# Hash attention and Fourier mixing on one Trainium2 core: the first weight's column means taken in one run through DRAM, the first pair's keys loaded head by head, the projection asked for first, the first key-bit copies dealt out anew

## The chip, the cores and the metric

The kernel runs on one core of a Trainium2 chip. The metric is the device time of one launch in microseconds (us). A core has a matrix engine (TensorE, PE in the profile; its weight loads are PEld), a vector engine (VectorE, DVE), a scalar engine (ScalarE, ACT), GpSimd (POOL) and SyncE (SP), which here only issues DMA transfers. ACT and POOL issue some transfers too. Each engine runs its own list of instructions in order, and semaphores hold an instruction until its operands are ready.

## The reference

```python
def _attn_ref(q, k, v, proj):                       # q, k, v: (4, 8, 768, 64), proj: (64, 6)
    q_bits = np.einsum('bhsd,dk->bhsk', q, proj) > 0
    k_bits = np.einsum('bhsd,dk->bhsk', k, proj) > 0
    powers = 2 ** np.arange(n_bits)
    q_bucket, k_bucket = np.sum(q_bits * powers, axis=-1), np.sum(k_bits * powers, axis=-1)
    mask = q_bucket[:, :, :, None] == k_bucket[:, :, None, :]
    scores = np.where(mask, scale * np.matmul(q, k.transpose(0, 1, 3, 2)), -1e9)
    attn = softmax(scores)                          # denominator + 1e-09
    return np.matmul(attn, v)                       # -> x: (4, 768, 512)

def _moe_ref(x, w_ch1, w_ch2):                      # w_ch1: (512, 2048), w_ch2: (2048, 512), float64
    mixed = np.real(fft(fft(x, axis=1), axis=2))
    u = x + mixed
    un = (u - mean(u)) / sqrt(var(u) + 1e-06)       # over the last axis
    return u + np.maximum(un @ w_ch1, 0.0) @ w_ch2
```

## The kernel before, in words

There are two phases. The attention phase takes 16 pairs of heads (four batches of four pairs; `n` is the pair's number). The mixing phase then does the Fourier transforms and the two-layer network for the four batches. `_any_scores` is a second version for inputs with large scores, which is not entered with these inputs.

**A pair.** `load` fetches queries, keys and values. For every pair but the first, queries and keys come in 32-column strips (runs of 128 bytes), which DVE can transpose itself. For the first pair (`n == 0`) the rows come as they lie, with a head's row as a run of 256 bytes, half from SP's queue and half from ACT's, and PE transposes them (tiles `trq`, `trk`; `ident` is the identity); DVE and ACT copy the results to `qt` and `kt`. `prepare` also multiplies queries and keys by the projection (`pj`, filled by POOL from `pjr`), which gives `bits`; DVE thresholds them into `qb`; and six small copies put the key bits into `kk` (two halves for each head) and the second query half into `q1`. `scores` multiplies the bits (a mask term, line 848) and the true values (line 858) into one tile `sc`, and ACT takes the exponential into `pk`. `values` multiplies `pk` with `vn` into `oo`, and DVE adds the `pk` up in `acc` for the softmax's denominator.

**Steps beside a pair.** A pair has three passes (`v` = 0, 1, 2), each with the scores of two key blocks and then the values of the two blocks before. Between them `next(other)` runs one step of `weights1`, four steps a pair from pair 2 on. `weights1` fetches w1 (`zraw`, SP's queue) in 16 slices of 128 x 512, and turns float64 into float32 in two steps a slice (DVE lines 643, 647 and 657, ACT lines 651 to 654). After every fourth slice, with a block of 512 columns complete, `centred(f)` subtracts the column means (the network's input is normalised, so its mean can be taken out of the weight): `average` sums the four slices with `ones` on PE (tile `ws`, the four sums side by side in four groups of 32 rows), ACT copies the sums to `part`, a second product with the constant matrix `mean` adds the four parts and spreads the mean over all rows (tile `wm`), ACT copies it to `avg`, and DVE subtracts it from the four slices, two in a step (`centre`).

**What sets the order.** In the attention phase the order of the code is the order on PE, DVE, ACT, POOL and SP (`manual_schedule`). Score tiles and all other PSUM tiles of this phase take turns in three buffers. SP takes its transfers in order, and one that waits for its data or its buffer holds back those behind it. When w1's columns are centred, SP also stores parts of them (tile `ad`, line 1271) for the mixing phase.

**Start.** PE runs nine products with `mean` (tile `busy`) while the first loads are under way. POOL fills constants, copies `pjr` into `pj`, and then issues half of the second pair's loads of queries and keys.

Of the kernel before, what the change touches and what calls it, by code (L numbers as in the profile page):

```python
# [11 lines left out]
F32 = mybir.dt.float32  # L12
# [471 lines left out]
def _main(  # L484
# [55 lines left out]
    def load(n, names="qkv", second=nc.sync):  # L540
# [6 lines left out]
        for nm in names:  # L547
            src = {"q": q, "k": k, "v": v}[nm]
            tag, bufs = ("vn", 2) if nm == "v" else ("qkn", 4)
            tl = at_([P, S], F32, tag, f"{nm}n{n}", bufs)  # L550
            nat[nm, n] = tl
            if nm == "v" or n == 0:
                tc_ = tl.rearrange("p (c h d) -> p c h d", c=NT, h=2)
                for h in range(2):
                    s = src[b, 2 * t + h]
                    s = (
                        s.rearrange("(p c) d -> p c d", c=NT) if n == 0
                        else s.rearrange("(c p) d -> p c d", p=P)
                    )
                    (second if h else nc.sync).dma_start(tc_[:, :, h, :], s)  # L560
                continue
            for i in range(4):
                s = src[b, 2 * t + i // 2, :, i % 2 * 32 : i % 2 * 32 + 32]
                d = tl[32 * i : 32 * i + 32]
                if nm == "k":
                    (nc.gpsimd if n == 1 and i % 2 else nc.sync).dma_start(
                        d.rearrange("p (j a) -> p j a", a=32),
                        s.rearrange("(j b) a -> b j a", b=32),
                    )
                else:  # L570
                    s = s.rearrange("(j b r) a -> r b j a", b=32, r=2)
                    d = d.rearrange("p (r j a) -> r p j a", r=2, a=32)
                    for r in range(2):
                        (nc.gpsimd if n == 1 and r else nc.sync).dma_start(d[r], s[r])
# [16 lines left out]
    nc.gpsimd.memset(pj, 0.0)  # L591
    pjr = const.tile([P, NBITS], F32, tag="pjr", name="pjr")
    for h in range(2):
        nc.sync.dma_start(pjr[h * D : (h + 1) * D], proj)
    for io, i in ((0, 0), (0, 1), (1, 0), (1, 2)):
        nc.gpsimd.tensor_copy(pj[:, io, 1 + i * NBITS : 1 + (i + 1) * NBITS], pjr)
    cmp_ = const.tile([P, 2, 2], F32, tag="cmp", name="cmp")
# [18 lines left out]
    for i in range(2):  # L616
        kks.append(att.tile([P, S], BF16, tag=f"kk{i}", name=f"kk{i}"))
        q1s.append(att.tile([P, HALF], BF16, tag=f"q1{i}", name=f"q1{i}"))
        nc.gpsimd.memset(kks[i], 0.0)
        nc.gpsimd.memset(q1s[i], 0.0)  # L620
    sq = const.tile([P, 2, 2, HALF + 1], F32, tag="sq", name="sq")
    ch = const.tile([P, 2, 2, DM // 2], F32, tag="ch", name="ch")
# [43 lines left out]

    def average(f):


        ps = pt([P, WC], f"ws{f}")  # L670
        for c in range(NDC):
            nc.tensor.matmul(
                ps[32 * c : 32 * c + 32, :], ones, w1[:, c, f : f + WC],
                start=True, stop=True,
            )
        part = wt([P, WC], F32, "u", f"part{f}", 2)
        nc.scalar.copy(part, ps)
        yield
        ps = pt([P, WC], f"wm{f}")
        nc.tensor.matmul(ps, mean, part, start=True, stop=True)  # L680
        avg = wt([P, WC], F32, "u", f"avg{f}", 2)
        nc.scalar.copy(avg, ps)
        yield avg

    def centre(f, avg, cs):
        for c in cs:
            w = w1[:, c, f : f + WC]
            nc.vector.tensor_tensor(w, w, avg, op=ALU.subtract)

# [51 lines left out]

    def centred(f):

        avg = average(f)
        next(avg)
        yield
        ps = next(avg)
        yield
        for c in range(0, NDC, 2):
            centre(f, ps, (c, c + 1))  # L750
            yield

    def weights1():
# [7 lines left out]
        for i in range(len(slices)):  # L761
            low = wt([P, WC], I32, "u", f"low{i}")
            yield from arrival.convert(i, low)
            yield
            if i % NDC == NDC - 1:
                yield from centred(fs[i // NDC])

# [4 lines left out]
    def prepare(n):  # L772

        ts = {}
        for nm in "qk":
# [9 lines left out]
            for g in range(2) if n == 0 else ():  # L785
                ps = pt([P, 3, P], f"tr{nm}{n}_{g}")
                for i in range(3):
                    c = 2 * i + g if nm == "q" else 3 * g + i
                    nc.tensor.transpose(ps[:, i, :], tn[:, c * P : (c + 1) * P], ident)
                if nm == "q":  # L790
# [27 lines left out]
        for h in range(2):  # L818
            nc.vector.tensor_scalar(
                bits[:, h], pss[h], cmp_[:, h, 0:1], cmp_[:, h, 1:2],  # L820
                op0=ALU.is_gt, op1=ALU.mult,
            )
        for h in range(2):
            to = slice(64 * h, 64 * h + 32)
            rest = [(kk[to, 0:HALF], 2), (kk[to, HALF:S], 3), (q1[to], 1)]
            for dst, i in rest:
                i ^= 2 * h
                (nc.scalar.copy if h else nc.vector.tensor_copy)(
                    dst, bits[32 * i : 32 * i + 32, h]
                )  # L830
        preps[n] = ts["q"], ts["k"], (bits, q1), kk
# [38 lines left out]
    def values(n, c, pk, oos):  # L870

        for g in range(2):
            w = HALF + 1 - g
            for h in range(2):
                nc.tensor.matmul(  # L875
                    oos[g][h * D : (h + 1) * D, 0:w], nat["v", n][:, (2 * c + h) * D : (2 * c + h + 1) * D],
                    pk[:, g, h, 0:w], start=(c == 0), stop=(c == NT - 1),
# [1014 lines left out]
```

## Time and profile before

| | |
|---|---|
| median of 3 runs | 998.35 us (997.3 to 999.73) |
| the profiled execution | 997.41 us, of which 995.3 us is the span of the instructions |
| mean granted clock of TensorE | 0.999 |
| busy: PE, DVE, ACT, POOL | 983.4, 724.7, 481.7, 96.6 us |
| attention phase | from the start to about 338 us |

The span runs from the first to the last instruction; the 2.1 us left of the profiled execution lie around it. A view called the chain follows the work that ended last back from the end, and names what each piece waited for. Rows of the timeline give start, length, engine, line, tile and, in brackets, idle time before it and who ended it. A row with x16 stands for 16 instructions. A product in float32 shows as two passes on PE, so 4 products show as x8.

### The profile page before, as it was taken

The page shows a single profiled execution, that of the slowest core. Times are in us where ns is not written, and L with a number is a line of the kernel's source. Part 1 is how long each engine was busy: PE and PEld are TensorE (multiplying, and loading weights), DVE is VectorE, ACT ScalarE, POOL GpSimd, SP SyncE. Part 2 cuts the span into 40 slices and gives each one's busy share as a digit, 9 for nine tenths or more (in the row PEclk, how much of TensorE's full clock was granted, in tenths as well). Part 3 has the DMA queues.
Part 4 walks back from the last instruction along what each step waited for, and adds up shares of the span by engine and source line. Part 5 has one row for each costly group of instructions (what it writes and reads, how often), then busy time and mean ns, then how long its engine had stood idle before and what let it go on. Part 6 is the DMA issues. An engine that isn't in the chain of part 4 may idle for free.

```text
span 995.3 us, 15351 instructions
## 1 busy us (share of the span) xinstructions
PE 983.4 (99%) x5505; PEld 692.0 (70%) x5505; DVE 724.7 (73%) x1276; ACT 481.7 (48%) x933; POOL 96.6 (10%) x193
## 2 busy tenths in 40 slices
PE   8999999999999999999999999999999999999997
PEld 5444444444444666875896686799989999998986
DVE  4788898878987597877835487547898857793672
ACT  5787887878866466047034423221643531430420
POOL 3000000000000000421212130002310001200000
PEclk9999999999999999999999999999999999999999
DMA  9545373453620337576663577205848612743701
GB/s 143 128 91 111 77 164 68 96 112 85 142 57 17 125 105 265 178 225 217 210 231 116 159 236 278 79 16 179 269 131 267 203 38 75 250 126 105 229 33 46
DMA packets 207141, 141.37 MB, mean 142 GB/s; under 512 B 128464, under 2 KB 190416, under 8 KB 207056
## 3 DMA queue, kind: packets, MB, share of 16 engines
q1 hardware_dynamic: 196464, 106.48, 38.9%
q0 software_dynamic: 9024, 33.43, 10.9%
q8 instruction: 46, 0.75, 0.3%
q10 hardware_dynamic: 1568, 0.39, 0.2%
q14 instruction: 39, 0.32, 0.1%
HBM read 111.94 MB, written 28.31 MB: 141 GB/s over the span
## 4 chain that ended last, share of the span: by engine, by line
PE 92%; DVE 3%; DMA 2%; ACT 1%; POOL 1%; issue 1%; SPq 0%; DVEq 0%; POOLq 0%
PE o L1400 29%; PE oo L875 13%; PE h L1750 13%; PE sc L858 12%; PE h_px L1514 6%; PE h_p L1514 5%; PE sc L848 4%; PE cs L1073 3%; PE A L1102 2%; PE B L1102 2%; DMA zraw<-in_moe_w_ch_dram 1%; PE sum L895 1%; PE bits L812 1%; PE un L1192 1%; DVE x L1116 0%
## 5 line engine op out<-in xcount | busy, mean ns | idle before, releaser
L1400 PE MATMUL o<-w,h 128*128 128x256 f32 x768 | 177.6, 379 | 0.0
L865 ACT ACTIVATE pk<-sc 128x768 f32<-128x768 f32 x192 | 152.5, 813 | 34.9 <-PE sc L858 31.4
L1400 PEld LDWEIGHTS o<-w,h 128*128 128x128 f32 x768 | 145.2, 190 | 19.0
L858 PE MATMUL sc<-qt,kt 64*128 64x384 f32 x768 | 155.6, 482 | 0.0
L875 PE MATMUL oo<-pk,vn 128*64 128x385 f32 (+1 forms) x768 | 134.5, 492 | 0.0
L932 DVE TENSOR_TENSOR acc<-acc,pk 128x1536 f32<-128x1536 f32 x63 | 110.1, 1748 | 3.1
L875 PEld LDWEIGHTS oo<-pk,vn 128*64 128x64 f32 x768 | 50.9, 136 | 81.0 <-issue 79.1
L1400 PE MATMUL o<-w,tq 128*128 128x256 f32 x384 | 91.1, 380 | 0.4 <-DVE w L1412 0.4
L858 PEld LDWEIGHTS sc<-qt,kt 64*128 64x128 f32 x768 | 69.6, 189 | 30.5 <-issue 30.0
L1400 PEld LDWEIGHTS o<-w,tq 128*128 128x128 f32 x384 | 72.5, 190 | 11.2 <-DVE w L1412 1.3
L1426 ACT COPY tq<-o 128x256 f32<-128x256 f32 x24 | 8.9, 372 | 141.0 <-PE o L1400 141.0
L1412 DVE SCALAR_TENSOR_TENSOR w<-o,rs,w 128x256 f32<-128x256 f32 x88 | 41.5, 480 | 40.2 <-PE o L1400 39.5
L1750 PE MATMUL h<-sums,w 128*128 128x192 f32 x336 | 61.6, 330 | 0.0
L1750 PEld LDWEIGHTS h<-sums,w 128*128 128x128 f32 x336 | 55.0, 190 | 2.9 <-DVE h L1688 2.0
L848 PEld LDWEIGHTS <-kk 33*128 33x128 bf16 x384 | 19.7, 93 | 50.8 <-issue 28.6
L1750 PE MATMUL h<-x,w 128*128 128x192 f32 x256 | 49.5, 326 | 0.0
L1435 ACT COPY tq<-o 128x256 f32<-128x256 f32 x24 | 8.9, 372 | 74.9 <-PE o L1400 74.9
L1750 PEld LDWEIGHTS h<-x,w 128*128 128x128 f32 x256 | 42.9, 190 | 0.1
L1400 PE MATMUL o<-w 128*128 128x256 f32 x176 | 41.7, 380 | 0.5 <-DVE w L1381 0.5
L1750 PE MATMUL h<-w 128*128 128x192 f32 x192 | 38.5, 327 | 0.0
L1688 DVE TENSOR_TENSOR h<-h,h 128x384 f32<-128x384 f32 x52 | 27.8, 551 | 14.5 <-PE h L1750 13.2
L1685 ACT ACTIVATE h<-h 128x768 f32<-128x768 f32 (+1 forms) x40 | 27.7, 712 | 20.3 <-DVE h L1688 19.6
(210 smaller groups left out, 1639.7 us busy)
## 6 DMA issues: line engine op xcount, KB each, us to landing
w<-ad SPq DMA_DIRECT2D x252, 128.0 KB, 2.6
w<-bd SPq DMA_DIRECT2D x42, 512.0 KB, 4.8
zraw<-in_moe_w_ch_dram SPq DMA_DIRECT2D x16, 512.0 KB, 4.5
zraw<-in_moe_w_ch_dram POOLq DMA_DIRECT2D x16, 512.0 KB, 4.0
bd<-w SPq DMA_DIRECT2D x14, 512.0 KB, 4.6
vn<-in_v_dram SPq DMA_DIRECT2D x32, 192.0 KB, 3.1
qn<-in_q_dram SPq DMA_DIRECT2D x116, 48.0 KB, 3.3
kn<-in_k_dram SPq DMA_DIRECT2D x58, 96.0 KB, 3.0
```

What stands on the lines that cost most here:

```text
L848: nc.tensor.matmul(pss[g][:, h, 0:HALF], kk[r, ks], bits[1][r] if g else bits[0][r, h], start=start, stop=not start,)
L858: nc.tensor.matmul(pss[g][:, h, 0:HALF], kt[rows, ks], qt[rows, g * HALF : (g + 1) * HALF], start=early, stop=not early,)
L865: nc.scalar.activation(pk[:, g, :, 0:HALF], pss[g][:, :, 0:HALF], AF.Exp, scale=SCALE)
L875: nc.tensor.matmul(oos[g][h * D : (h + 1) * D, 0:w], nat["v", n][:, (2 * c + h) * D : (2 * c + h + 1) * D], pk[:, g, h, 0:w], start=(c == ...
L932: nc.vector.tensor_tensor(acc, (first[:, :, :, 0:HALF] if c == 1 else acc), new, op=ALU.add)
L1073: nc.tensor.matmul(ps[:, pc + 2 * lo : pc + 2 * hi - 1 : 2], z[:, cp, pc, par, t * P : (t + 1) * P], ch[:, cp, pc, lo:hi], start=(cp == 0) ...
L1102: nc.tensor.matmul(ps[:, cols], F[:, par, k, t, j * P : (j + 1) * P], sq[:, t, k, cols], start=(t == 0), stop=(t == 1),)
L1400: nc.tensor.matmul(ps, a[:, r], right7[i][:, r], start=start and r == 0, stop=r == HF // 2 - 1, skip_group_check=not start,)
L1412: done_by[ET.DVE] = nc.vector.scalar_tensor_tensor(t[:, cols], src, r, t[:, cols], op0=ALU.mult, op1=ALU.add)
L1514: nc.tensor.matmul(ps, left[:, k], right[i][:, k], start=start and k == 0, stop=k == 1, skip_group_check=not start,)
L1688: done_by[ET.DVE] = nc.vector.tensor_tensor(d, x, y, op=ALU.add)
L1750: nc.tensor.matmul(ps[at_bank][:, g], ring[n % NR][:, g], parts[i][j], start=start and g == 0, stop=g == 1, skip_group_check=True,)
```

## The change

Four edits.

1. `centred` is called once, after all 16 slices are converted. It sums all 16 slices in one run of 16 products into one tile (the four column blocks side by side, accumulated over the four slices of each), ACT copies the sums scaled by 1/512 to `part`, SP writes the four rows of means to a DRAM tile `md`, and each block's means come back spread over all 128 rows by a DMA into `avg`. The first two are asked for in the step after the write, three steps ahead of their use, the other two when the subtractions of the block two before are done. DVE subtracts one slice in a step. The product with the constant matrix and the second ACT copy are gone.
2. The first pair's keys, and the values of all pairs, lie head by head in SBUF. For the first pair each head's rows for keys and values are then runs of 1536 bytes (queries as before). The keys are transposed by twelve plain products of a 64-column stationary (the keys) with `ident`, the two heads in two column groups, in the place of six transposes of 128 columns.
3. The projection `pjr` is fetched by POOL, right after its first constant, and no longer by SP behind the first queries and keys. POOL copies it into `pj` after all its constants.
4. Of the six small copies of the first pair, ACT does two for head 0 (the first key half, then `q1`) and DVE does the other four (head 1 first, the second key halves last). For other pairs only the order of the three copies of a head changes.

The core of the diff:

```diff
-                tc_ = tl.rearrange("p (c h d) -> p c h d", c=NT, h=2)
                 for h in range(2):
...
+                    s, half = src[b, 2 * t + h], tl[:, h * HALF : (h + 1) * HALF]
+                    if nm == "q":
+                        half = tl.rearrange("p (c h d) -> p c h d", c=NT, h=2)[:, :, h]
+                        s = s.rearrange("(p c) d -> p c d", c=NT)
+                    elif n == 0:
+                        s = s.rearrange("(p c) d -> p (c d)", c=NT)
...
+                    (second if h else nc.sync).dma_start(half, s)
...
-    nc.gpsimd.memset(mean, 1.0 / (32 * DM))
+    nc.gpsimd.memset(mean, 1.0)
+    pjr = const.tile([P, NBITS], F32, tag="pjr", name="pjr")
+    for h in range(2):
+        nc.gpsimd.dma_start(pjr[h * D : (h + 1) * D], proj)
...
-    for h in range(2):
-        nc.sync.dma_start(pjr[h * D : (h + 1) * D], proj)
...
+    def centred():
+        nf = DFF // WC
+        ps = pt([P, WC], "sums")
+        for c in range(NDC):
+            for i in range(nf):
+                nc.tensor.matmul(
+                    ps[32 * i : 32 * i + 32, :], ones, w1[:, c, i * WC : (i + 1) * WC],
+                    start=c == 0, stop=c == NDC - 1,
+                )
+        part = wt([P, WC], F32, "u", "part", 2)
+        nc.scalar.activation(part, ps, AF.Copy, scale=1.0 / DM)
+        yield
+        md = tc.dram_tile([nf, WC], F32, name="md")
+        nc.sync.dma_start(md, part[0:P:32])
+        yield
...
+                nc.sync.dma_start(
+                    avgs[i], bass.AP(row.tensor, row.offset, [[0, P], [1, WC]])
+                )
...
+        for i in range(nf):
+            for c in range(NDC):
+                w = w1[:, c, i * WC : (i + 1) * WC]
+                nc.vector.tensor_tensor(w, w, avgs[i], op=ALU.subtract)
+                yield
+            fetch(i + 2)
...
+                    for h in range(2):
+                        nc.tensor.matmul(
+                            ps[h * D : (h + 1) * D, i, :],
+                            tn[:, (h * NT + c) * D : (h * NT + c + 1) * D], ident,
+                            start=True, stop=True,
+                        )
...
+            rest = [(kk[to, 0:HALF], 2), (q1[to], 1), (kk[to, HALF:S], 3)]
+            copies += [(dst, 32 * (i ^ 2 * h), h, i) for dst, i in rest]
+        if n == 0:
+            copies.append(copies.pop(2))
+        for dst, at, h, i in copies:
+            by_act = h if n else not h and i < 3
+            (nc.scalar.copy if by_act else nc.vector.tensor_copy)(dst, bits[at : at + 32, h])
```

PE at the end of pair 9, where before the third of the four groups of sums stood (names as in the words above; `oo` are the values):

```order
L858 MATMUL sc_1_5_1917<-qt_1607,kt_1609 128x384 x2
L672 MATMUL ws_1930<-w_134,ones 32x512 x4
L875 MATMUL oo_0_1784<-pk_116,vn_1601 64x385 x2
L875 MATMUL oo_1_1785<-pk_116,vn_1601 64x384 x2
L875 MATMUL oo_0_1784<-pk_118,vn_1601 64x385 x2
```

and now, at the same place:

```order
L874 MATMUL sc_1_5_1922<-qt_1615,kt_1617 128x384 x2
L676 MATMUL sums<-w_134,ones 32x512 x16
L891 MATMUL oo_0_1791<-pk_112,vn_1609 64x385 x2
L891 MATMUL oo_1_1792<-pk_112,vn_1609 64x384 x2
L891 MATMUL oo_0_1791<-pk_114,vn_1609 64x385 x2
```

The other three groups of four sums (in pairs 3, 6 and 12) and the four products `wm` (in the first pass of pairs 4, 7, 10 and 13) are gone from PE's list; the rest of its attention phase stands as before.

SP's list about pair 10 before (`qn`, `kn`, `vn` are loads of pairs to come):

```order
L560 DMA vn_1959<-in_v_dram 128x6x64 x2
L574 DMA qn_2125<-in_q_dram 32x12x32 x8
L566 DMA kn_2134<-in_k_dram 32x24x32 x4
L1271 DMA ad<-w_134 256x1x128 x8
L560 DMA vn_2139<-in_v_dram 128x6x64 x2
```

and now:

```order
L563 DMA vn_1976<-in_v_dram 128x6x64 x2
L684 DMA md<-part 4x512
L692 DMA avg_2053<-md 128x512
L692 DMA avg_2055<-md 128x512
L577 DMA qn_2136<-in_q_dram 32x12x32 x8
L569 DMA kn_2145<-in_k_dram 32x24x32 x4
L563 DMA vn_2150<-in_v_dram 128x6x64 x2
L577 DMA qn_2307<-in_q_dram 32x12x32 x8
L569 DMA kn_2316<-in_k_dram 32x24x32 x4
L1287 DMA ad<-w_134 256x1x128 x8
```

The write of the means and two fetches stand ahead of the loads for pair 13, the first stores `ad` come a pair later, and the w1 slices are fetched without pauses and so earlier.

DVE at the start before (the first pair's keys, thresholds and small copies, then the second pair's transposes):

```order
L533 COPY kt_154<-trk_0_155 128x384
L819 TENSOR_SCALAR qb_165<-bits_166,cmp 128x384 x2
L828 COPY kk_124<-qb_165 32x384 x2
L828 COPY q_125<-qb_165 32x384
L784 STREAM_TRANSPOSE qt_242<-qn_183 128x2x2x192
```

and now:

```order
L533 COPY kt_154<-trk_0_155 128x384
L832 TENSOR_SCALAR qb_171<-bits_172,cmp 128x384 x2
L846 COPY kk_120<-qb_171 32x384
L846 COPY q_121<-qb_171 32x384
L846 COPY kk_120<-qb_171 32x384 x2
L789 STREAM_TRANSPOSE qt_248<-qn_189 128x2x2x192
```

DVE has one copy more, with `q1` second; ACT has one copy less there.

More of the change, by code (lines that the diff above doesn't have):

```diff
@@ L740, in slices1 @@
         ]
[L742 to L751, printed above, removed]
     def weights1():
```

55 lines of the change are left out of this document (19 added, 36 removed).

## The prediction

> **What bounds the kernel now.** I read the page's head first, then stretches of the attention phase, then the chain there, then the timeline of the first 20 us.
>
> ```profile
> span 995.3 us, 15351 instructions
> PE 983.4 (99%) x5505; PEld 692.0 (70%) x5505; DVE 724.7 (73%) x1276; ACT 481.7 (48%) x933; POOL 96.6 (10%) x193
> 20.00:340.00 320.00, 320.00 (x2283) 139.29 (x2280) 268.76 (x348) 241.37 (x414) 0.11 (x1) 1.00 0.43 91
> 60.00:80.00 20.00, 20.00 (x147) 8.70 (x144) 18.42 (x24) 17.43 (x31) 0.00 (x0) 1.00 0.52 113
> ```
>
> A stretch row gives its length, then the busy time of PE, PEld, DVE, ACT and POOL, then granted clock, DMA share and GB/s. From 20 to 340 us PE is busy without a gap at clock 1.00, so what PE no longer does there comes off the time, as long as no other engine gets late. The second row is the fullest stretch for DVE, with two w1 slices converted in a pair: 18.42 of 20 us, and PE still full.
>
> **Edit 1, the column means.** The chain, rows of start, length and piece; x2 and x8 count passes.
>
> ```profile
> 84.97 0.99 PE ws L672 x8
> 92.05 1.06 PE wm L680 x2
> 93.11 2.73 PE oo L875 x16
> ...
> 270.19 0.99 PE ws L672 x8
> 277.27 1.05 PE wm L680 x2
> 324.11 0.78 PE sum L895 x8
> 336.30 1.43 PE sum L895 x16
> ```
>
> First and last of four each. Each `wm` lies on the chain with `oo` at its end, so four of them give back 4 x 1.06 = 4.2 us. The groups of sums now stand in one run. The rows for `sum` price that: the same stationary, four column groups of 32, and eight passes more cost 1.43 - 0.78 = 0.65 us for 384 columns, hence 0.87 for 512. One run of 32 passes is 0.99 + 3 x 0.87 = 3.6 us against 4 x 0.99 = 4.0: 0.4 us saved. Sum of edit 1 on PE: 4.6 us. The lower end is the four `wm` alone, 4.2 us.
>
> What it adds lies elsewhere. DVE subtracts 16 slices as before. ACT loses seven copies and keeps one. The conversions, now without pauses from pair 2 to pair 9, load eight pairs like the stretch from 60 to 80 us, where DVE keeps 1.6 us spare and PE does not wait; if that cover went, each microsecond over 20 in a pair would be a microsecond on PE. The means' way through DRAM has no row of its own. Its place does:
>
> ```profile
> 219.35 0.98 SPq L560 DMA_DIRECT2D vn<-in_v_dram  x2
> 238.36 0.68 DVE L657 CUSTOM_DVE_ANT_0 w<-w,low 128x1024 uint16<-128x1024 uint16 x1
> w<-ad SPq DMA_DIRECT2D x252, 128.0 KB, 2.6
> w<-bd SPq DMA_DIRECT2D x42, 512.0 KB, 4.8
> ```
>
> The write stands on SP behind these `vn`, so it is issued at about 220.3 on the clock of before; the first subtraction stands on DVE where the conversion at 238.36 stood. The last two rows bound a transfer from DRAM (KB, us to landing): write and fetch in turn take 2 x 2.6 to 2 x 4.8 us, and with some 2 us of issue the means are there by 228 to 232. I take the later, since a spread read touches all rows: 6 us to spare. Behind the waiting fetch on SP stand the queries and keys of pair 13, which DVE transposes in pair 12, a pair after; ten microseconds' delay leaves them early. The other two fetches are asked for a pair's quarter behind the subtractions that free their buffer, four steps ahead. I cost all of this at nothing.
>
> **Edits 2 to 4, the start.** The timeline from 0 to 20 us, in order of time:
>
> ```profile
> 0.98 3.70 PE L580 MATMUL busy<-mean 128*128 128x128 f32 x18 [0.98 <-POOL warm L583]
> 6.93 0.85 PE L789 MATMUL trk<-ident,kn 128*128 128x128 f32 x6 [1.00 <-DMA kn<-in_k_dram]
> 7.47 0.56 POOL L596 COPY pj<-pjr 128x6 f32<-128x6 f32 x4 [5.04 <-DMA pjr<-in_proj_dram]
> 7.81 0.48 ACT L535 COPY kt<-trk 128x384 f32<-128x384 f32 x1 [0.99 <-PE trk L789]
> 9.28 1.26 DVE L819 TENSOR_SCALAR qb<-bits,cmp 128x384 bf16<-128x384 f32 x2 [1.24 <-PE bits L812]
> 9.46 2.71 POOL L574 DMA_DIRECT2D qn<-in_q_dram  x4
> 10.57 0.74 DVE L828 COPY kk<-qb 32x384 bf16<-32x384 bf16 x2
> 10.63 1.04 ACT L828 COPY kk<-qb 32x384 bf16<-32x384 bf16 x2 [2.34 <-DVE qb L819]
> 11.35 0.29 DVE L828 COPY q<-qb 32x384 bf16<-32x384 bf16 x1
> 12.15 1.42 POOL L566 DMA_DIRECT2D kn<-in_k_dram  x2
> 12.26 0.32 PE L848 MATMUL sc<-q,kk 33*128 33x384 bf16 x1 [0.25 <-ACT q L828]
> 17.28 0.98 DVE L784 STREAM_TRANSPOSE kt<-kn 128x768 f32<-128x768 f32 x1 [0.52 <-DMA kn<-in_k_dram]
> 17.38 0.83 PE L812 MATMUL bits<-qt,pj 64*32 64x384 f32 x2
> 18.31 0.87 PE bits L812 x14
> 305.04 0.81 PE bits L812 x16
> ```
>
> The chain through this is short to tell: `pjr` lands, POOL fills `pj`, then issues the second pair's loads; their keys land at 17.2, are transposed, and PE, which stood at the second pair's `bits` from 17.38, goes on at 18.31. After 19.18 PE is never free again. So what the start is worth is how much earlier PE gets past these `bits`.
>
> *Small copies (edit 4).* The last mask product of the first two score tiles starts at 12.26, waiting for ACT's third copy; ACT starts only when both thresholds (1.26 us, so 0.63 each) are done. Now ACT starts after the first threshold, at 9.28 + 0.63 + 0.1 (the gap to ACT's start now) = 10.0, and with two copies of 0.52 is done at 11.05. DVE does one key half (0.37) and `q1` (0.29) of head 1 after both, done at 10.57 + 0.66 + 0.1 = 11.3. The last mask starts 0.95 us earlier. The two second key halves are wanted three key blocks later and DVE has them 0.75 us after.
>
> *The second pair (edit 3).* A pair's `bits` take 0.81 us; from 17.38 to 19.18 they took 1.80, so the wait for keys cost 1.0 us. POOL issued these loads from 9.46. Now its list ahead of them is two small transfers, the same constants, and the copies. Two issues at 0.7 (2.71/4) put the constants back by 1.4 us; these took until 2.4 (7.47 less 5.04 idle), and the fills between copies and loads 1.4 more (8.03 to 9.46), so all end by 5.3; `pjr` lands some 4 us after its issue,
>
> ```profile
> qn<-in_q_dram POOLq DMA_DIRECT2D x4, 48.0 KB, 3.6
> pjr<-in_proj_dram SPq DMA_DIRECT2D x2, 1.5 KB, 4.4
> kn<-in_k_dram SPq DMA_DIRECT2D x1, 192.0 KB, 5.3
> 3.00:4.00 1.00, 1.00 (x7) 1.00 (x6) 0.00 (x0) 0.58 (x2) 0.00 (x0) 1.00 1.23 277
> 5.00:6.00 1.00, 0.85 (x6) 0.64 (x6) 0.36 (x2) 0.00 (x0) 0.00 (x0) 1.00 1.24 181
> ```
>
> so by 6.0 to 6.9, copies end by 7.5, and the loads start near 7.6 at the latest, 1.9 us earlier. SP's half also moves up by two issues. Keys are then transposed by 16.4 (17.28 + 0.98 - 1.9), and PE comes to them at 17.38 - 0.95 + 0.3 (below) = 16.7. The 1.0 us goes. If POOL were as late as before, PE would wait for keys at the same 18.31 and both gains would be lost.
>
> *The first keys (edit 2).* PE waits for them until 6.93. In the last two rows DMA moves 277 GB/s and then only 181 while keys are on the way. What takes a microsecond at 181 takes 0.65 at 277, so about 0.35 us could go if longer runs hold the higher rate to the end; I take 0.5, since the keys also were in flight beside short runs before that, between nothing and 1.0. Against that, the transposes. Six took 0.85 us. Twelve plain products are 24 passes. Lower end, with heads side by side and streaming alone, 12 x 0.11:
>
> ```profile
> 679.25 0.87 PE un L1192 x8
> L875 PEld LDWEIGHTS oo<-pk,vn 128*64 128x64 f32 x768 | 50.9, 136 | 81.0 <-issue 79.1
> ```
>
> (0.87/8 = 0.11 a pass of 128 columns) is 1.3 us. Upper end, no load of 64 columns (136 ns) beside another: 24 x 0.136 = 3.3. `busy` lies between: 18 passes in 3.70 us, 0.206 each, the load of 128 columns being what sets the pace; half of it for each head gives 24 x 0.103 = 2.5 if loads queue. In the `oo` row above, 16 passes of 64-column stationaries in 2.73 us are 0.34 a pair of heads, where 384 columns stream in 0.325 (0.65/2), so the loads of one head hide behind the other's streaming. I take 1.8 us, between 1.3 and 2.5. The last key copy then starts at 6.93 - 0.5 + 1.8 = 8.2 and not 7.81, and `bits` end 0.3 to 0.4 us later: 0.3 lost, between 0.6 gained (1.0 sooner and 1.3 us) and 2.4 lost. The projection, which let the first `bits` go only at 7.8 to 8.0, is out of the way by 7.5.
>
> The Trainium skill, "TensorE: Matmul & The Clock Gate", section "Part 3: Packing small matmuls — row/col tiling", says that weight loads overlap running products only when the row group differs; here both heads use all rows and differ by columns, so by it no load would hide. By it the sum would be 3.4 us saved (second price of the first rival below) and not 6.2. The `oo` row disagrees: 16 loads of 0.136 unhidden would be 2.2 us of its 2.73.
>
> **Sum.** 4.6 + 0.95 + 1.0 - 0.3 = 6.2 us. From the profiled execution's 997.4 that is 991.2; the median of the runs stands 0.9 higher, which gives 992.1. I forecast 991.7 between them.
>
> **The rivals.** *The start gives nothing.* The keys' transposes cost 2.5 us and more, or POOL's loads stay late, and all 1.95 us go. For it: no row shows a 64-column product with so short a stream. Against it: `oo`. Then 4.6 less a few tenths, from 998.35: 994.0. With no load hidden behind a stream, 3.3 + 1.3 = 4.6 us of transposes in the place of 1.8, the sum is 6.2 - 2.8 = 3.4: 994.9. Chance 0.17.
>
> *DVE becomes the bound: slower.* In pairs 2 to 9 DVE carries 18.42 us in 20, and a PE third without `wm` is 1.06 us shorter every third pair, so DVE has less. It decides once a pair's DVE work passes PE's 20 us; with 1.5 us over in eight pairs, 12 - 6 = 6 us lost: 1004. Against it: the 1.6 us spare. Chance 0.03.
>
> *The saving does not reach the end.* After attention the chain goes over a transfer of the second weight:
>
> ```profile
> 337.73 7.24 PE cs L1073 x48
> 345.25 4.49 DMA zraw<-in_moe_w_ch_dram
> ```
>
> Were it bound to a clock of its own, PE would wait there for what it saved, 998. But it starts as PE's `cs` ends and moves with it. Chance 0.05.
>
> **How the numbers follow.** Likeliest case 0.75, the three rivals 0.17, 0.03 and 0.05. A measurement tells about 0.2%, 2 us, from no change. Faster by more: the likeliest case and most of the first rival, 0.90; same 0.07; slower 0.03. The range: the best bounds give 4.6 + 0.95 + 1.0 + 0.6 = 7.2, 990.2 from the profiled time, and 0.9 of scatter makes 989.3; upwards it takes in the first rival with 0.6 of scatter, 995.1.
>
> **What would show it.** No row for `wm`; one run `sums` of 3.6 us; PE full from 20 to 340 us; DVE subtractions that wait for no DMA. At the start, the last mask product near 11.5, the second pair's `bits` unbroken and ending near 17.5, `trk` 1.3 to 2.5 us long. Wrong would be DVE or SP rows among what PE waits for after 20 us, or `bits` of the first pair ending after 10.5.

## The result and the profile after

| | before | after |
|---|---|---|
| median of the runs | 998.66 us | 991.38 us |
| ratio, 95% interval | | 0.9928 (0.9911 to 0.9946) |
| the profiled execution, its span | 997.41, 995.3 us | 991.51, 989.4 us |

A second measurement of the changed kernel, described with the experiments, gave 991.91 against 998.45 us, 0.9933 (0.992 to 0.9946). The 998.66 us are the three runs of before that were known ahead (998.35) and a fourth. The forecast was 991.7.

The head of the page of after, and three of its stretches (length, then busy time of PE, PEld, DVE, ACT and POOL):

```profile
span 989.4 us, 15387 instructions
PE 978.8 (99%) x5515; PEld 690.7 (70%) x5515; DVE 724.6 (73%) x1277; ACT 476.9 (48%) x925; POOL 97.8 (10%) x195
20.00:340.00 320.00, 320.00 (x2308) 143.75 (x2307) 268.57 (x348) 240.74 (x419) 1.23 (x3) 1.00 0.45 102
60.00:80.00 20.00, 20.00 (x148) 8.78 (x148) 18.44 (x24) 17.40 (x31) 0.00 (x0) 1.00 0.53 114
280.00:300.00 20.00, 20.00 (x148) 8.78 (x146) 18.82 (x29) 13.14 (x23) 0.00 (x0) 1.00 0.18 48
```

PE is busy for 4.6 us less (983.4 before), and in the attention phase it is as full as it was. That this equals the 4.6 us forecast for edit 1 confirms nothing: the means alone, below, show 980.6 us and the start alone 984.1, so busy totals do not price the edits, and the chain has to. DVE is as busy from 60 to 80 us as it was. Its fullest stretch is now a later one, from 280 to 300 us (16.71 us before), and PE has no gap there either.

The chain of before at three more places, and then the chain of after (start, length, piece):

```profile
19.19 2.74 PE oo L875 x16
...
400.10 32.64 PE o L1400 x150
472.91 34.80 PE o L1400 x160
```

```profile
16.69 0.81 PE bits L825 x16
17.50 2.74 PE oo L891 x16
202.76 3.57 PE sums L676 x32
331.36 7.24 PE cs L1089 x48
338.88 4.46 DMA zraw<-in_moe_w_ch_dram
393.70 32.64 PE o L1416 x150
467.08 34.80 PE o L1416 x160
```

Read as a clock, it shows where the time came from. The first values `oo` start 1.69 us earlier (19.19 to 17.50). By the Fourier products `cs` the lead is 6.37 us (337.73 to 331.36), and the 4.68 us that came on top are the column means. At the first outer products `o` it is 6.40, at the second 5.83, at the end of the span 5.9.

The start of after, in order of time (start, length, engine, line, what; in brackets the idle time before it and who ended it):

```profile
1.30 1.29 POOL L583 DMA_DIRECT2D pjr<-in_proj_dram  x2 [0.38 <-issue]
6.29 0.56 POOL L623 COPY pj<-pjr 128x6 f32<-128x6 f32 x4 [0.73 <-DMA pjr<-in_proj_dram]
6.51 1.53 PE L798 MATMUL trk<-ident,kn 128*64 128x128 f32 x24 [0.62 <-DMA kn<-in_k_dram]
7.01 2.50 POOL L577 DMA_DIRECT2D qn<-in_q_dram  x4
11.59 5.95 ACT L881 ACTIVATE pk<-sc 128x768 f32<-128x768 f32 x8 [0.23 <-PE sc L864]
15.48 0.98 DVE L789 STREAM_TRANSPOSE kt<-kn 128x768 f32<-128x768 f32 x1 [1.07 <-DMA qn<-in_q_dram]
```

POOL's loads for the second pair start at 7.01 instead of 9.46 us, the transpose of that pair's keys at 15.48 instead of 17.28, and the second pair's `bits` run unbroken (0.81 us in the chain). The keys of the first pair let PE begin 0.42 us sooner (6.93 before), and their 24 passes take 1.53 us.

### The profile page after: what moved, and what is told of

The parts are those of the page before. It is cut to its first block, busy times and chain, and to the rows that moved or that the text cites. A ratio compares the mean times of both kernels' runs of the same rounds, so it can differ in the third digit from the quotient of the medians.

```text
span 989.4 us, 15387 instructions
## 1 busy us (share of the span) xinstructions
PE 978.8 (99%) x5515; PEld 690.7 (70%) x5515; DVE 724.6 (73%) x1277; ACT 476.9 (48%) x925; POOL 97.8 (10%) x195
## 4 chain that ended last, share of the span: by engine, by line
PE 92%; DVE 3%; DMA 2%; ACT 1%; issue 1%; POOL 0%; SPq 0%; POOLq 0%; DVEq 0%
PE o L1416 29%; PE oo L891 13%; PE h L1766 13%; PE sc L874 13%; PE h_px L1530 6%; PE h_p L1530 5%; PE sc L864 4%; PE cs L1089 3%; PE A L1118 2%; PE B L1118 2%; DMA zraw<-in_moe_w_ch_dram 1%; PE bits L825 1%; PE sum L911 1%; PE un L1208 1%; DMA ad<-qs 1%
```

## The experiments

All kernels here compute the whole output. The table collects, from the chain of each profile, when the first `oo` starts (PE is past the second pair's `bits`), when `cs` starts (end of attention), and how long after `cs` the outer products of the first half (x150) and then of the second half (x160) start. The last column is the ratio of the timed runs to those of the kernel before on the same chip, or, for a single look, its time in us.

| kernel | first `oo` | `cs` | `oo` to `cs` | `cs` to x150 | x150 to x160 | ratio or us |
|---|---|---|---|---|---|---|
| before | 19.19 | 337.73 | 318.54 | 62.37 | 72.81 | 1 |
| after | 17.50 | 331.36 | 313.86 | 62.34 | 73.38 | 0.9928 |
| after, again | 17.70 | 331.56 | 313.86 | 62.82 | 72.77 | 0.9933 |
| means only | 19.23 | 333.12 | 313.89 | 63.14 | 72.80 | 0.9954 |
| start only | 17.41 | 335.93 | 318.52 | 64.33 | 73.91 | 0.9996 |
| start only, again | 17.56 | 336.12 | 318.56 | 63.51 | 74.18 | 0.9985 |
| keys as before | 18.05 | 331.96 | 313.91 | 63.06 | 72.49 | 992.0 |
| projection as before | 19.32 | 333.23 | 313.91 | 62.45 | 72.98 | 993.25 |
| copies as before | 18.83 | 332.70 | 313.87 | 63.39 | 73.00 | 993.45 |
| projection, early copies | 18.45 | 332.36 | 313.91 | 62.48 | 72.97 | 992.5 |
| no lead | 17.65 | 334.53 | 316.88 | 62.96 | 72.73 | 994.48 |
| after, later bits | 17.61 | 331.49 | 313.88 | 61.85 | 72.73 | 0.9926 |
| start only, later bits | 17.47 | 336.00 | 318.53 | 61.83 | 73.45 | 0.9979 |
| before, later bits | 19.80 | 338.37 | 318.57 | 62.27 | 72.66 | 0.9990 |

### The means alone

The kernel before with edit 1 only, `centred` as in the diff of the change, called once:

```diff
-            if i % NDC == NDC - 1:
-                yield from centred(fs[i // NDC])
+        yield from centred()
```

> The kernel before with edit 1 alone (the means in one run through DRAM). My theory, that PE is the bound all through attention and edit 1 takes 4.6 us from its list: span 995.3 - 4.6 = 990.7, time 994.0 from a median of 998.6, ratio 0.9954. In the chain the last sums of attention begin 4.6 us earlier than before, with the second pair's projections ending where they did, near 19.2. Rival, that the start makes most of the result and edit 1 gives part of its gain back in the mixing phase (later stores of the first weight): 996 or more, the gain at the end of attention being larger than at the end of the span by 2 us.

Measured: 993.68 against 998.23 us, ratio 0.9954 (0.994 to 0.9967). Its chain:

```profile
333.12 7.24 PE cs L1075 x48
340.64 5.22 DMA zraw<-in_moe_w_ch_dram
396.26 32.64 PE o L1402 x150
```

The end of attention is 4.61 us earlier than before, the 4.6 us of the sum. In this one execution 0.8 us were gone again at the outer products (400.10 to 396.26 us), behind a transfer that took 5.22 us where it took 4.49 before; the timed runs kept 4.5.

### The start alone

The changed kernel with `centred` as before, so edits 2, 3 and 4 only:

```diff
-        yield from centred()
+            if i % NDC == NDC - 1:
+                yield from centred(fs[i // NDC])
```

> The changed kernel with edit 1 undone (sums and means by two products for each block, as before). My theory, that the start is worth 1.7 us by itself and adds to the means: span 993.6, time 996.9, ratio 0.9983; the second pair's projections end at 17.5 without a wait. Rival, that a start that is earlier only meets a later wait for loads in attention: second pair's projections at 17.5, but the end of attention less than 1 us earlier than before and the time 998.

Measured: 998.03 against 998.23 us, ratio 0.9996 (0.9987 to 1.0005). From its chain:

```profile
335.93 7.24 PE cs L1087 x48
343.45 6.41 DMA zraw<-in_moe_w_ch_dram
400.26 32.64 PE o L1414 x150
```

This was a miss in the end time and not in the mechanism: PE was past the start 1.78 us earlier and ended attention 1.80 us earlier. Then the first transfer of the second weight landed 6.41 us after its issue, 4.49 before, and the outer products started where they had started before. That place is taken up below.

### One edit of the start undone at a time

Each of these is the changed kernel with one edit taken back. Keys (edit 2): rows interleaved as for the queries, six transposes of 128 columns.

```diff
-                    if nm == "q":
+                    if nm in "qk":
```

> The changed kernel with the first pair's keys loaded in runs of 256 bytes and transposed by six transposes, as before (the values stay head by head). My theory, that the twelve products cost more (1.5 against 0.85 us) than the longer runs bring (keys at 6.5 and not 6.9): keys at 6.8, the first pair's projections end near 9.2 and not 9.47, the second pair's near 17.2 and not 17.5. Rival, that the longer runs are what clears the DMA queues for the second pair: keys at 6.9 or later, the second pair's keys land later than 16 and its projections end at 17.8 or later.

Projection (edit 3): on SP's queue, copies ahead of the memsets.

```diff
-    for h in range(2):
-        nc.gpsimd.dma_start(pjr[h * D : (h + 1) * D], proj)
...
+    for h in range(2):
+        nc.sync.dma_start(pjr[h * D : (h + 1) * D], proj)
+    for io, i in ((0, 0), (0, 1), (1, 0), (1, 2)):
+        nc.gpsimd.tensor_copy(pj[:, io, 1 + i * NBITS : 1 + (i + 1) * NBITS], pjr)
```

> The changed kernel with the projection fetched by SP behind the first queries and keys and copied by POOL ahead of its last fills, as before. My theory, that POOL's wait for the projection is what made the second pair's loads late: POOL's loads start near 9.2 and not 7.0, PE waits some 1 us for the second pair's keys and its projections end at 18.5. Rival, that the loads got faster because the first keys and values are fewer, longer runs, whoever fetches the projection: POOL's loads start late but land soon, and the second pair's projections end by 17.8.

Copies (edit 4): ACT takes all three of one head, DVE those of the other.

```diff
-            by_act = h if n else not h and i < 3
+                (nc.scalar.copy if h else nc.vector.tensor_copy)(
```

> The changed kernel with the copies of key bits as before (part 4 undone: in the first pair ScalarE takes three copies in a row, the last mask copy ends about 0.95 us later; in every later pair one more copy is VectorE's). Theory 1 (the first pair's scores and exponentials wait for the last copy): exponentials of the first pair and the second pair's bits 0.5 to 1.0 us later than in the changed kernel, bits end at 18.0 to 18.5 us against 17.50, and the whole attention behind it by as much; the dense stretches as they are (VectorE under 18.8 us of 20). Rival (the second pair's loads set these bits, the last copy has cover): end 17.4 to 17.7, no loss.

Projection, split in two: fetched by POOL first as in the changed kernel, but POOL's four copies of it stand ahead of three of the masks' memsets again.

```diff
+    for io, i in ((0, 0), (0, 1), (1, 0), (1, 2)):
+        nc.gpsimd.tensor_copy(pj[:, io, 1 + i * NBITS : 1 + (i + 1) * NBITS], pjr)
...
-    for io, i in ((0, 0), (0, 1), (1, 0), (1, 2)):
-        nc.gpsimd.tensor_copy(pj[:, io, 1 + i * NBITS : 1 + (i + 1) * NBITS], pjr)
```

> The changed kernel with the projection fetched by GpSimd first as there, but GpSimd's four copies of it into the stationary tile back ahead of the masks' memsets: the copies wait for the transfer until 6.3 us, three memsets of 1.64 us together come behind them, then GpSimd's loads for the second pair (7.01 us in the changed kernel). Theory 1 (what counts of the projection's move is when GpSimd can begin with its loads): loads at 8.5 to 8.8 us, the second pair's queries land 1 to 1.7 us later, the second pair's bits end at 18.3 to 19.0 us against 17.50. Rival (what counts is that the projection has left SyncE's queue): bits end 17.4 to 17.8.

The decisive rows of the four timelines, in the order keys, projection, copies, split:

```profile
6.95 0.56 POOL L623 COPY pj<-pjr 128x6 f32<-128x6 f32 x4 [1.39 <-DMA pjr<-in_proj_dram]
7.12 0.85 PE L794 MATMUL trk<-ident,kn 128*128 128x128 f32 x6 [0.98 <-DMA kn<-in_k_dram]
7.67 2.49 POOL L577 DMA_DIRECT2D qn<-in_q_dram  x4
16.14 0.98 DVE L789 STREAM_TRANSPOSE kt<-kn 128x768 f32<-128x768 f32 x1 [1.24 <-DMA qn<-in_q_dram]
```

```profile
6.35 0.56 POOL L599 COPY pj<-pjr 128x6 f32<-128x6 f32 x4 [3.93 <-DMA pjr<-in_proj_dram]
8.34 2.71 POOL L577 DMA_DIRECT2D qn<-in_q_dram  x4
11.06 6.15 ACT L881 ACTIVATE pk<-sc 128x768 f32<-128x768 f32 x8 [0.23 <-PE sc L864]
17.41 0.98 DVE L789 STREAM_TRANSPOSE kt<-kn 128x768 f32<-128x768 f32 x1 [1.94 <-DMA kn<-in_k_dram]
```

```profile
12.28 0.51 ACT L841 COPY q<-qb 32x384 bf16<-32x384 bf16 x1
12.81 6.06 ACT L878 ACTIVATE pk<-sc 128x768 f32<-128x768 f32 x8
```

```profile
8.38 2.50 POOL L577 DMA_DIRECT2D qn<-in_q_dram  x4
16.54 0.98 DVE L789 STREAM_TRANSPOSE kt<-kn 128x768 f32<-128x768 f32 x1 [0.87 <-DMA kn<-in_k_dram]
```

The keys' landing on the chain of the projection kernel, and then on that of the split one:

```profile
11.74 5.59 DMA kn<-in_k_dram
```

```profile
11.58 4.88 DMA kn<-in_k_dram
```

Each of the four was looked at once, so the scatter of the start has to be known. The start of the changed kernel stands unaltered in seven profiles of the table (after twice, start only twice, no lead, and two with later bits); there the first `oo` starts at 17.41 to 17.70 us. The losses below are against the one profile of after; against its repeat they are 0.2 us smaller.

- *Projection.* Undone, it costs 1.87 us at `cs`, all that the three edits bring together. POOL's loads start 1.3 us later, the second pair's keys are transposed at 17.41, and PE waits for them although the first pair was even earlier (exponentials at 11.06 instead of 11.59). The expectation missed in size: it had the loads start near 9.2 us and these `bits` end at 18.5, and it was 8.34 and 19.32. The split kernel loses 1.0 us with POOL's loads 1.4 us later, as its first theory had it: about half of this edit is POOL's order and not SP's queue. For the other 0.9 us POOL's start is not the reason, since it is as late in both kernels; 0.7 us of it is the keys' landing, 5.59 against 4.88 us. Without any edit of the start this landing took 4.34, 4.41 and 4.92 us. Whether SP's queue or chance made it longer here was not tested.
- *Copies.* Undone, 1.34 us: ACT's third copy starts at 12.28 and the exponentials at 12.81, 1.2 us later. The keys of this execution also had PE start its first `bits` 0.3 us later. What the copies are worth shows from the start of the thresholds to that of the exponentials: 2.95 us in all four profiles with the old copies, 2.04 to 2.33 in the ten with the new ones, so 0.6 to 0.9 us. The rival (cover by the second pair's loads) fell.
- *Keys.* Undone, 0.60 us, where 17.2 us had been expected for the end of these `bits` and 18.05 came, as the rival had it. The first pair gains nothing from edit 2: keys land later, transposes are shorter, and the exponentials start at 11.51. The gain lies in the second pair: POOL's copies of the projection wait for it until 6.95 us, against 6.29 in after and 6.29 to 6.67 in the seven profiles, and POOL's loads and the transpose of that pair's keys follow as much later. So 0.3 to 0.7 us, from one profile. A second pair of kernels points the same way: with SP fetching the projection from 2.4 us on, it was there at 7.43 to 7.50 us beside the short runs (before, means only, before with later bits) and at 6.35 beside the long ones, which keys and values have there (projection as before). The short runs delay the small transfer that is in flight with them.

The three losses add up to 3.8 us (3.2 against the repeat of after), while the three edits together are worth 1.8. PE goes on where two streams have both arrived, the first pair's scores and the second pair's keys, and holding back either one loses the gain of the other.

### No lead for the means

The changed kernel without the three steps between the fetch and the first subtraction.

```diff
-        for _ in range(3):
-            yield
```

> The changed kernel with the three steps between asking for the column means and the first subtraction left out: the first subtractions stand on VectorE behind the addition that ended at 215.1 us, while the means were asked for at 218.8 us and land some 3.6 to 4.4 us later. Theory 1 (the three steps cover the round trip; VectorE's slack of 1.6 us in 20 cannot): VectorE waits 7 to 8 us for the means, the next pair's key bits start as much later, TensorE waits 3 to 7 us, end of attention 3 to 7 us later than 331.36, ratio about 0.996 to 1.0, so most of the means' gain is gone. Rival (TensorE has enough products queued ahead of what VectorE releases): TensorE waits under 1 us, time as in the changed kernel.

Its chain, its timeline of DVE, and the stretch around it:

```profile
216.42 2.51 DMA md<-part
218.98 3.40 DMA avg<-md
```

```profile
222.47 1.29 DVE L701 TENSOR_TENSOR w<-w,avg 128x512 f32<-128x512 f32 x2 [7.25 <-DMA avg<-md]
```

```profile
220.00:240.00 20.00, 17.51 (x120) 7.74 (x114) 17.09 (x22) 10.52 (x20) 0.00 (x0) 1.00 0.36 73
```

DVE waits 7.25 us for the means, PE loses 2.5 of them in that stretch, and attention takes 3.0 us longer from `oo` to `cs`: two thirds of the means' gain is gone. PE's own loss is at the lower edge of what was expected (3 to 7 us), since it had work queued: DVE stands from 215.2 us on, and PE's first gap, 0.42 us, ends at 224.31. The lead is needed, and its cover shows too: the means land at 222.4, and in the changed kernel the first subtraction starts here:

```profile
233.15 0.69 DVE L703 TENSOR_TENSOR w<-w,avg 128x512 f32<-128x512 f32 x1
```

So 10 us were to spare.

### Where the start's gain went: the second weight's first transfer

In the mixing phase DVE converts the second weight between its additions into `x`. Its first conversion stands behind the additions of the first of four columns and waits for the transfer; the additions of the other three columns, and PE's transposes of `x` behind them, wait with it. Four kernels were timed together: the changed kernel and the start alone, each as it is, and each with this conversion one step later.

```diff
-            if i >= n and (i - n) % 2 == 0:
+            if i >= n and (i - n) % 2 == 0 and i != skip or i == skip + 1 > 0:
...
-            other = after(NT - 2, other, islice(arrival2, HF + 2))
+            other = after(NT - 2, other, islice(arrival2, HF + 2), NT)
```

> The changed kernel itself, unaltered, with the kernel before on the same chip, to have it beside the start alone and the variants below. Theory 1 (the gains of means, 4.6 us, and start, 1.7 us, add up, and the transfers in the mixing phase only add scatter of about one us): ratio 0.9937, 992.0 to 992.3 us against 998.3; the first transfer of the second weight lands anywhere between 4.4 and 6.4 us after its issue. Theory 2 (the mixing phase takes back what the start gains, in every execution, unless the means have moved too): ratio 0.9928 as in the first measurement, first transfer again in 4.5 us.

> The start's three edits alone (projection on GpSimd's queue, keys head by head, copies split) once more, means as before: in the first measurement the 1.8 us that the trace showed at the end of attention were gone 60 us later, behind a transfer of the second weight that landed in 6.41 us instead of 4.49 us. Theory 1 (that landing scatters from execution to execution): this profile lands in 4.4 to 5.3 us, outer products from 398.3 to 399.1 instead of 400.3, and the median of the runs is 996.7 to 997.5. Theory 2 (it belongs to this order of instructions): it lands in 6.2 to 6.6 us again, median 998.0.

> The changed kernel, but the first conversion of the second weight is taken one step later in the mixing phase (behind the additions into x of the second column instead of the first), the second one with the next step as before. Theory 1 (VectorE stands in order behind a transfer there, 0.83 us in the changed kernel's profile and 0.83 to 2.8 us in others, and TensorE's transposes wait for x behind it): VectorE's wait for this transfer goes to 0 to 0.3 us, the transposes and outer products start 0.2 to 0.6 us earlier than in the changed kernel, the runs scatter less, median 0.2 to 0.8 us lower. Rival (VectorE's work there is as much as TensorE's, and conversions pushed together only move the wait to the first hidden products, which need x less x first): no change or up to 1 us slower.

> The start's three edits alone, means as before, and the same later conversion as in the kernel ahead of this. Theory 1 (the wait for the second weight's first transfer took back the start's 1.8 us): outer products 1.5 to 2.0 us earlier than in the start alone, 398.3 to 398.7; median 1.3 to 2.0 us below that of the start alone, ratio to before 0.9978 to 0.9985. Rival (something else behind it takes it back, in the second half of the block between 430 and 470 us): outer products near 398.5 but the end as in the start alone, ratio 0.9993 to 1.0.

The first conversion on DVE in the start alone, again, and then in the changed kernel with the later conversion:

```profile
349.27 0.43 DVE L646 TENSOR_SCALAR w<-zraw 128x512 int32<-128x512 int32 x1 [1.99 <-DMA zraw<-in_moe_w_ch_dram]
```

```profile
345.18 0.42 DVE L646 TENSOR_SCALAR w<-zraw 128x512 int32<-128x512 int32 x1
```

Measured: after 991.91 us (0.9933), start alone 996.95 (0.9985, 0.9976 to 0.9994), after with the later conversion 991.14 (0.9926, 0.9913 to 0.9939), start alone with it 996.09 (0.9979, 0.997 to 0.9988).

What the wait costs shows when the chains are laid beside the table's column `cs` to x150. The transfer's length and that column are 4.46 and 62.34 us in after, 4.49 and 62.37 before, 5.22 and 63.14 with the means only, 6.41 and 64.33 with the start only: the difference is 57.9 us each time, and so it is in all nine profiles whose chain has this transfer. Each microsecond of it is a microsecond on PE. The wait is gone in both edited kernels, and the outer products come 61.8 us after `cs`, against 62.3 to 64.3 in all kernels without this edit; by the same sum that is a transfer of some 4.0 us. On the clock of the start alone that is 1.8 us earlier (399.63 to 397.83). The transfer scatters: the start alone landed in 6.41 us at first and in 5.6 now, between its two theories (4.4 to 5.3, 6.2 to 6.6), the changed kernel in 4.46 and then in about 5.0 (DVE waited 0.83 and 1.33 us). These two of the start alone are the longest of all, so a share of its order of instructions is not ruled out. The repeat also moved the start alone from 0.9996 to 0.9985, with most of its gain showing. For the changed kernel 0.9933 lies between both theories and tells nothing apart. The changed kernel with the later conversion is the fastest version here: 0.8 us below the changed kernel on the same chip, its five runs within 0.3 us of one another, although the two intervals overlap. The other kernels with it still scatter by 1.7 and 1.8 us.

The end time of the start alone fell only 0.9 us with the later conversion, where 1.3 to 2.0 had been expected. The table says where the rest is: between the two halves' outer products the three profiles with the start alone take 73.45 to 74.18 us, the others 72.49 to 73.38.

A last run took the later conversion alone, on the kernel before, as the partner of the start alone with it.

> The kernel before, with nothing of the change but the later conversion of the second weight, as the partner of the start alone with that conversion (ratio 0.9979). Theory 1 (the start is worth its 1.8 us wherever the wait for the second weight's first transfer is out of the way, and this conversion alone is worth 0.5 to 0.9 us, as it was on the changed kernel, 991.14 against 991.91): VectorE's wait for that transfer is gone, outer products start 0.2 to 0.8 us earlier than 400.1, ratio 0.9991 to 0.9996, so that the start's part of 0.9979 is 1.2 to 1.7 us. Rival (the later conversion did it all, and the start gives next to nothing at the end of the program): ratio 0.9979 to 0.9985.

Measured: 997.63 against 998.65 us, ratio 0.9990 (0.9981 to 1.0). Its chain:

```profile
338.37 7.22 PE cs L1073 x48
400.64 32.64 PE o L1400 x150
```

The ratio is a little below the expected 0.9991 to 0.9996, and the rival's 0.9979 to 0.9985 lies at the lower end of its interval. What is left for the start is 0.9979/0.9990, or 1.1 us, just under the expected 1.2 to 1.7 and with an uncertainty as large as itself, since both ratios carry some 0.9 us either way. The outer products are not earlier than 400.1 us, as had been expected: in this execution the start, which has nothing changed, took until 19.80 instead of 19.19 us. Counted from `cs` they come 62.27 us later, 0.1 less than in the profile of before and 0.4 more than in the other two kernels with this conversion. The first wait is gone here too, but DVE waits for a later transfer of the same weight:

```profile
371.52 0.43 DVE L643 TENSOR_SCALAR w<-zraw 128x512 int32<-128x512 int32 x1 [0.70 <-DMA zraw<-in_moe_w_ch_dram]
```

That the conversion did not do it all is likely, then, and not shown; how much of the 1.8 us the start keeps at the end without the means' edit is known only to about a microsecond.

## Why the prediction was right

- *Edit 1, 4.6 us.* Right, in size too. Fourteen profiles in the table have 318.5 us from `oo` to `cs` without it and 313.9 with it (317 without the lead): 4.65 us. The run of sums was put at 3.6 us and is 3.57.
- *The means' way through DRAM costs nothing.* Right; the 6 us to spare were mis-sized. From the write's issue to the means' landing the prediction had 7.7 to 11.7 us (220.3 to 228 or 232) and took the longer. In the kernel without the lead it was 6.0 (216.42 to 222.38), and some 10 us were left. The spread read was feared to cost more than a plain load; in after these reads landed in 3.6 to 4.4 us, inside the 2.6 to 4.8 that the prediction had for a transfer:

```profile
DMA to landing us min/median/max: 3.6/4.1/4.4
```

- *Copies, 0.95 us, less 0.3 for the keys.* Right in mechanism and in the difference of the two: exponentials start 0.64 us earlier. Each term alone is at its upper end: the copies are worth 0.6 to 0.9 us, and the thresholds start 0.27 us later in this profile (9.28 to 9.55), but at 9.23 to 9.55 in the seven profiles with this start, against 9.28 to 9.37 in the three without.
- *Projection, 1.0 us.* Right, and it carries the others: without it none of the start's gain is left, as the prediction's sentence "If POOL were as late as before, PE would wait for keys at the same 18.31 and both gains would be lost" says. Loads were forecast to start by 7.6 and start at 7.01. That they set the keys' landing one for one is not so: with the projection as before they started 1.1 us earlier than in the kernel before (8.34, 9.46), and the keys were transposed no earlier (17.41, 17.28).
- *Keys.* The parts were right (0.5 us sooner, was 0.42; 1.8 us of transposes, was 1.53; `bits` 0.3 later, were 0.3 later in this profile), and the verdict was incomplete. The sum books this edit as a loss of 0.3 us. Undone, it loses 0.4 to 0.6, since its longer runs also speed the projection, on which POOL and the second pair depend. The prediction had that chain and those runs, and did not join them.
- *The saving reaches the end.* The rival that the transfer of the second weight holds PE to a clock of its own is right in no kernel; the transfer's issue always follows `cs` by 7.5 us. But its landing scatters by 2 us, and PE pays for what exceeds some 4.0 us. That was not in the sum, where scatter stood only at the ends of the range. The two measured gains, 7.3 and 6.5 us, are above the 5.9 between the two profiled executions, since the profile of before was a quick execution (997.41 against a median of 998.66).
- *The other rivals.* DVE never became the bound: its fullest stretch has 18.82 us of 20 and PE no gap. That the start gives nothing fell by the changed kernel's `oo` at 17.50 and by the ratios: 0.9928 and 0.9933 with it on top of the means, 0.9954 without. The top of the forecast's range, 995.1, does not follow from its own terms (the first rival's 994.0 or 994.9 with 0.6 of scatter are 994.6 or 995.5); nothing here hangs on it.
- *The rule on packed weight loads.* The Trainium skill, "TensorE: Matmul & The Clock Gate", "Part 3: Packing small matmuls — row/col tiling", lets weight loads overlap running products only where the row group differs, in one of its points, and in another also where the load goes to a background weight buffer. By the first the transposes would have taken the prediction's 3.3 + 1.3 = 4.6 us. They took 1.53 us, 64 ns a pass with all rows in use and the heads side by side in columns, and the 24 loads of 0.137 us in them make 3.3 us, so this trace disagrees with the first point and not with the second.

What stays open is the stretch between the halves. All three profiles of the start alone lose another 0.6 to 1.4 us there against the kernel before, and after loses 0.6. These four, and no other of the fourteen, have a transfer of the second weight on their chain there that starts 118.7 to 121.5 us after `cs`; in the others the last one starts by 114.4. From the start alone and from after:

```profile
456.94 5.00 DMA zraw<-in_moe_w_ch_dram
452.88 5.63 DMA zraw<-in_moe_w_ch_dram
```

So this wait does not belong to the start alone. It wasn't shown whether the order of the transfers or chance makes it late.

## What to carry to other kernels

Where an engine goes on only after two streams have met, undoing one edit at a time overstates each: here the parts lost 3.2 to 3.8 us where the whole is worth 1.8. Look for instructions that stand in order behind a transfer with work of others queued behind them: one step later the medians of three kernels were 0.8 to 1.0 us lower, with overlapping intervals, for no work saved. And follow a gain from place to place along the chain (`oo`, `cs`, `o`) before trusting its end time, since one profile can lose 2 us to a late transfer.

## What the hardware showed that was not expected

The keys' transposes, products of 64-column stationaries with the two heads side by side in columns, ran at 64 ns a pass (1.53 us for 24), where a lone pass over 128 columns is 0.11 us (0.87 us for the eight of the `un` row). One after the other the two heads' passes would take 0.22 us, and they took 0.128. So they streamed at the same time, and with their weight loads, by which the prediction put the transposes at up to 2.5 us, they took 0.2 us more than the bare 1.3.

Rates of a start's loads depend on the mix in flight. From 5 to 6 us the changed kernel moves 342 GB/s, the same kernel with short runs for the keys 224, and the kernel before 181 (338 to 350 in the seven profiles with the changed start):

```profile
5.00:6.00 1.00, 0.90 (x7) 0.66 (x6) 0.39 (x2) 0.00 (x0) 0.56 (x2) 1.00 1.10 342
```

```profile
5.00:6.00 1.00, 0.90 (x7) 0.64 (x6) 0.15 (x1) 0.00 (x0) 0.56 (x2) 1.00 1.36 224
```

The Trainium skill, "DMA: Bandwidth & Descriptors", "Why small descriptors are slow (HBM only)", gives a descriptor of 256 bytes an overhead of 27%. The loads of the two changed kernels differ in the keys' runs alone, 1536 bytes against 256, and the rate is a third lower with the short ones, so the trace agrees in direction. What mattered for the time was the small transfer beside them, which landed 0.3 to 0.7 us later.
